# Storing each 128-token output tile with one DMA in place of four

## The chip, the cores and the metric

The kernel runs on one core of a Trainium2 chip. Times are device microseconds (us) of one execution, and each time quoted is the median of all executions of that kernel in its rounds. A span is the length of one profiled execution as the profiler sees it, 1.8 to 2.1 us below the device time of the same execution; all profiled executions shown were in the fast state. In the views, PE is TensorE (PEld its weight loads), DVE is VectorE, ACT is ScalarE, POOL is GpSimd and SP is SyncE; a q after the name is that engine's queue of instructions. PSUM is the memory that holds the tiles named ps_ in the views, which the matmuls write.

## The reference, cut to what matters

```
p_packed = softmax(p k^T / 8) v             # per batch and head: 32 x 64
attn     = softmax(q p_packed^T / 8) p_packed
x        = attn as 4608 tokens x 512        # 8 batches x 576 tokens
out      = relu(x @ w_in)**2 @ w_out        # 4608 x 512 float32, 9.44 MB
```

Only the last line's output and its way to memory are touched by the change.

Of the kernel before, what the change touches and what calls it, by code (L numbers as in the profile page):

```python
# [18 lines left out]
JT = 18  # L19
# [84 lines left out]
def kernel_impl(tc, q, k, v, p, w_in, w_out, out):  # L104
    nc = tc.nc
    B, H, S, Dh = q.shape
# [11 lines left out]
    NT = TOK // P  # L118

    with ExitStack() as ctx:  # L120
# [41 lines left out]
        def cast(eng, dst, src):  # L162
            if eng is nc.scalar:
                nc.scalar.copy(dst, src)  # L164
            else:
                eng.tensor_copy(dst, src)  # L166
# [290 lines left out]
        EH = NE // 2  # L457
# [16 lines left out]
        def out_tile():  # L474
            return opool.tile([P, 2, NE], F32, name="o_sb")

        def store(t, src, eng=None, e0=0, e1=NE):
            for i in range(4):
                b, j = divmod(t * 4 + i, JT)
                dst = out[b * S:(b + 1) * S, e0:e1].rearrange("(a j) e -> j a e", j=JT)[j]  # L480
                (eng or nc.sync if i % 2 else nc.sync).dma_start(dst, src[32 * i:32 * i + 32])
# [8 lines left out]
        def f2_last_out(hf, eng):  # L490
            if hf == 0:
                ob[NT - 1] = out_tile()
            o = ob[NT - 1][:, hf, :EH]
            cast(eng, o, po[NT - 1, hf][:, :EH])
            store(NT - 1, o, nc.scalar, hf * EH, (hf + 1) * EH)

        def f2_mm(t, fb):
            n0 = (t * P) % (2 * S)
# [5 lines left out]
        def f2_out(t, eng):  # L504
            ob[t] = out_tile()
            o = ob[t][:, 0]
            cast(eng, o, po[t])
            store(t, o)
# [53 lines left out]
        def prod_out(t, n, eng):  # L562
            ps = po[t, n not in (2, 4, 6)].rearrange("p (u e) -> p u e", u=2)
            if n == 1:
                ob[t, 0] = out_tile()
            if n == 4:
                ob[t, 1] = out_tile()
            o = ob[t, 0 if n in (1, 2, 3, 6) else 1]
            o = o[:, :, :EH] if n in (1, 2, 7) else o[:, :, EH:]
            if n in (1, 3, 4, 7):  # L570
                cast(eng, o, ps)
            else:
                eng.tensor_tensor(out=o, in0=ps, in1=o, op=ALU.add)  # L573
            if n in (6, 7):
                for u in range(2):
                    store(t + u + (2 if n == 7 else 0), ob[t, n - 6][:, u])
# [189 lines left out]
        def f2_last_steps():  # L766
            res = []
            t = NT - 1
            for hf in range(2):
                for fb in range(NFB):  # L770
                    st = [stage([("PE", 0.11, lambda fb=fb, hf=hf: f2_last(hf, fb))])]
                    end = fb == NFB - 1
                    if end:
                        st.append(stage([("DVE", 0.35, lambda: f2_last_out(0, V)) if hf == 0 else ("ACT", 0.38, lambda: f2_last_out(1, A))]))
                    res.append(Step(f"F2.{t}.{hf}.{fb}", st, g_ready([t], [fb]), [(bk(t, hf), 1)] if fb == 0 else [("osb", 1)] if end and hf == 0 else [],
                                    [(bk(t, hf), 1, f"F2.{t}.{hf}.0")] + ([("osb", 1, f"F2.{t}.0.{fb}")] if hf else []) if end else []))
            return res
# [154 lines left out]
```

## The kernel before: what the change touches

A q load puts token `a*18 + j` of a batch (a = 0..31, j = 0..17) on partition a, position j. A transpose on DVE then makes columns in the order `j*32 + a`. So a tile of 128 columns holds four values of j with 32 tokens each, and on the output side its 128 partitions are four groups of 32 rows; rows of one group are 18 rows apart in the output. The kernel stores each group by a DMA of its own:

```
S, JT, P, NE, EH = 576, 18, 128, 512, 256           # 36 tiles of 128 tokens
opool = tile_pool(name="opool", bufs=3)              # three output buffers of two tiles

def store(t, src, eng=None, e0=0, e1=NE):
    for i in range(4):
        b, j = divmod(t * 4 + i, JT)
        dst = out[b * S:(b + 1) * S, e0:e1].rearrange("(a j) e -> j a e", j=JT)[j]
        (eng or nc.sync if i % 2 else nc.sync).dma_start(dst, src[32 * i:32 * i + 32])
...
def f2_out(t, eng):                                   # tiles 0 to 14, one at a time
    ob[t] = out_tile(); o = ob[t][:, 0]
    cast(eng, o, po[t]); store(t, o)
...
# tiles 15 to 34: groups of four (15, 19, 23, 27, 31), seven products each; two tiles are
# stored after product 6 and two after product 7
# tile 35: in two halves of 256 columns, with nc.scalar for two of each half's four DMAs
```

SP (`nc.sync`) only issues DMAs. The order of all work on each engine is fixed in the kernel. All loads but three are issued by GpSimd (81 of 84). The page counts loads and stores together, in the DMA row's mean busy share of the core's 16 DMA engines.

The softmax here doesn't subtract the row's maximum and nothing guards it: scores larger than these inputs give would overflow.

## Time and profile before

| | before |
|---|---|
| device time, median of 3 runs | 250.09 us (248.85 to 252.26) |
| span of the profiled run (an execution of 251.01 us) | 249.2 us |
| TensorE (PE) busy | 226.0 us, 91% |
| last matmul ends | 241.71 us |
| stretch after it | 7.4 us |
| stores issued | 144 by SP, 4 by ACT |

The prediction shows most of the lines to read. Two more answers are needed for the comparison: the row of the table by stretches in which the loads end (columns: length; busy us and instructions of PE, PEld, DVE, ACT, POOL; clock; DMA share; GB/s), and the view of the output tensor, with the time that SP needs for an issue (min/median/max in ns).

```profile
60.00:80.00 20.00, 18.66 (x180) 10.21 (x182) 16.23 (x27) 16.30 (x30) 8.54 (x18) 1.00 1.05 174
...
L481 SPq DMA_DIRECT2D out_dram<-o_sb x144: 314/422/1790, 48.5 to 246.6; - x144
```

### The profile page before, as it was taken

The page shows a single profiled execution, that of the slowest core. Times are in us where ns is not written, and L with a number is a line of the kernel's source. Part 1 is how long each engine was busy: PE and PEld are TensorE (multiplying, and loading weights), DVE is VectorE, ACT ScalarE, POOL GpSimd, SP SyncE. Part 2 cuts the span into 40 slices and gives each one's busy share as a digit, 9 for nine tenths or more (in the row PEclk, how much of TensorE's full clock was granted, in tenths as well). Part 3 has the DMA queues.
Part 4 walks back from the last instruction along what each step waited for, and adds up shares of the span by engine and source line. Part 5 has one row for each costly group of instructions (what it writes and reads, how often), then busy time and mean ns, then how long its engine had stood idle before and what let it go on. Part 6 is the DMA issues. An engine that isn't in the chain of part 4 may idle for free.

```text
span 249.2 us, 5356 instructions
## 1 busy us (share of the span) xinstructions
PE 226.0 (91%) x2079; PEld 161.1 (65%) x2096; DVE 185.8 (75%) x325; ACT 158.0 (63%) x273; POOL 60.3 (24%) x120
## 2 busy tenths in 40 slices
PE   0667999999899999999999999999999999999980
PEld 0523745476544666666646778887787888888860
DVE  3774557895898896679787989988898798768410
ACT  2467556988687676776788788887875756400010
POOL 7596668473076003261010000000000000000000
PEclk9999999999999999999999999999999999999997
DMA  6999999999989963799711010033004101504243
GB/s 214 200 145 183 205 201 208 204 226 241 197 124 192 248 134 56 117 165 214 144 45 42 3 42 3 0 82 92 3 21 120 32 3 39 130 1 105 66 108 103
DMA packets 27160, 29.01 MB, mean 116 GB/s; under 512 B 5760, under 2 KB 18816, under 8 KB 27136
## 3 DMA queue, kind: packets, MB, share of 16 engines
q0 software_dynamic: 19472, 17.99, 45.7%
q1 hardware_dynamic: 7328, 9.97, 14.7%
q10 hardware_dynamic: 336, 0.72, 0.8%
q8 instruction: 16, 0.26, 0.4%
q14 instruction: 8, 0.07, 0.1%
HBM read 37.22 MB, written 9.44 MB: 187 GB/s over the span
## 4 chain that ended last, share of the span: by engine, by line
PE 74%; DMA 15%; POOL 3%; DVE 2%; issue 1%; ACT 1%; SPq 0%; POOLq 0%
PE ps_o L560 24%; PE ps_h L417 20%; PE ps_o L501 15%; DMA q_b<-in_q_dram 7%; DMA k_b<-in_k_dram 4%; DMA p_b<-in_p_dram 3%; PE ps_m L354 3%; PE ps_a L283 3%; PE ps_h L426 3%; PE ps_s L379 2%; POOL v_r L238 1%; PE ps_pp L316 1%; PE ps_s L391 1%; DVE qT L267 1%; DMA out_dram<-o_sb 1%
## 5 line engine op out<-in xcount | busy, mean ns | idle before, releaser
L445 ACT ACTIVATE r<-ps_h 128x576 bf16<-128x576 f32 x99 | 63.7, 650 | 26.6 <-PE ps_h L417 24.6
L417 PE MATMUL ps_h<-a,M 128*128 128x288 bf16 x448 | 71.0, 286 | 0.2
L501 PE MATMUL ps_o<-w_out_b,gT 128*128 128x512 bf16 x193 | 54.6, 379 | 0.9 <-issue 0.5
L417 PEld LDWEIGHTS <-M 128*128 128x128 bf16 x448 | 43.6, 98 | 16.3
L452 DVE TENSOR_TENSOR gT<-r 128x1152 bf16<-128x1152 bf16 x64 | 46.8, 748 | 6.8 <-ACT r L445 3.8
L560 PEld LDWEIGHTS <-wS 128*128 128x128 bf16 x320 | 31.0, 98 | 4.7 <-issue 0.4
L501 PEld LDWEIGHTS <-gT 128*128 128x128 bf16 x240 | 22.2, 98 | 17.0 <-issue 3.4
L560 PE MATMUL ps_o<-wT,wS 128*128 128x256 bf16 x240 | 30.4, 273 | 0.0
L164 ACT CAST M<-ps_m 128x1024 bf16<-128x1024 f32 (+1 forms) x26 | 23.0, 915 | 6.8 <-PE ps_m L354 4.9
L238 POOL DMA_DIRECT2D v_r<-in_v_dram x32 | 19.0, 598 | 33.3 <-DVE wT L525 16.9
L560 PEld LDWEIGHTS <-gT 128*128 128x128 bf16 x240 | 23.3, 98 | 3.8 <-issue 0.4
L267 DVE STREAM_TRANSPOSE qT<-q_b 128x1152 bf16<-128x1152 bf16 (+1 forms) x18 | 21.9, 1229 | 3.7 <-DMA q_b<-in_q_dram 3.5
L164 ACT COPY o_sb<-ps_o 128x512 f32<-128x512 f32 (+1 forms) x15 | 8.6, 572 | 22.7 <-PE ps_o L560 19.6
L560 PE MATMUL ps_o<-w_out_b,gT 128*128 128x256 bf16 x160 | 20.9, 273 | 0.0
L283 PE MATMUL ps_a<-pT_bd,kT 128*128 128x128 bf16 x128 | 11.0, 242 | 9.5 <-DVE kT L273 8.6
L166 DVE COPY o_sb<-ps_o 128x512 f32<-128x512 f32 (+1 forms) x20 | 13.4, 672 | 8.1 <-PE ps_o L560 3.6
L283 PEld LDWEIGHTS <-kT 128*128 128x128 bf16 x128 | 9.3, 109 | 11.9 <-DVE kT L273 9.0
L166 DVE CAST M<-ps_m 128x1024 bf16<-128x1024 f32 (+1 forms) x10 | 11.2, 1118 | 7.5 <-PE ps_m L354 6.8
L386 ACT ACTIVATE e<-ps_s,rD 128x576 bf16<-128x576 f32 (+1 forms) x18 | 12.2, 687 | 6.8 <-PE ps_s L379 6.8
L573 DVE TENSOR_TENSOR o_sb<-ps_o,o_sb 128x512 f32<-128x512 f32 x15 | 10.3, 690 | 6.2 <-PE ps_o L560 5.0
L379 PE MATMUL ps_s<-qT,pq_bd 128*128 128x288 bf16 x64 | 11.4, 304 | 2.8 <-DVE qT L267 1.5
L273 DVE STREAM_TRANSPOSE kT<-k_b 128x320 f32<-128x320 f32 (+1 forms) x32 | 13.1, 450 | 1.2 <-DMA k_b<-in_k_dram 0.9
(72 smaller groups left out, 304.4 us busy)
## 6 DMA issues: line engine op xcount, KB each, us to landing
out_dram<-o_sb SPq DMA_DIRECT2D x140, 64.0 KB, 1.7
k_b<-in_k_dram POOLq DMA_DIRECT2D x14, 288.0 KB, 8.5
q_b<-in_q_dram POOLq DMA_DIRECT2D x14, 288.0 KB, 8.7
v_r<-in_v_dram POOLq DMA_DIRECT2D x16, 160.0 KB, 8.2
v_r<-in_v_dram POOLq DMA_DIRECT2D x16, 128.0 KB, 7.4
w_in_b<-in_moe_w_in_dram POOLq DMA_DIRECT2D x8, 256.0 KB, 8.7
w_out_b<-in_moe_w_out_dram POOLq DMA_DIRECT2D x8, 256.0 KB, 9.2
k_f<-in_k_dram ACTq DMA_DIRECT2D x1, 576.0 KB, 4.7
```

The source lines that it names most:

```text
L164: nc.scalar.copy(dst, src)
L166: eng.tensor_copy(dst, src)
L238: nc.gpsimd.dma_start(self.vr[32 * i:32 * i + 32, h0:h1, :n * D], src[:, :, J0[i] * D:(J0[i] + n) * D])
L267: nc.vector.transpose(self.qT[:, qd, :, j0 * 32:j1 * 32].rearrange("p dh (j a) -> p j dh a", a=32), self.t.qb[qd][:, j0 * D:j1 * D].rearra ...
L273: nc.vector.transpose(self.kT[:, qd, :n * P].rearrange("p (g jp a) -> p jp g a", jp=4, a=32)[:, i:i + 2], self.t.kb[qd][:, J0[i] * D:(J0[i ...
L283: nc.tensor.matmul(ps[:, g * P:(g + 1) * P], lhsT=self.kT[:, qd, g * P:(g + 1) * P].bitcast(BF16).rearrange("p (t two) -> p two t", two=2) ...
L379: nc.tensor.matmul(ps[:, c], lhsT=self.pq[:, blk(qd, dh)], rhs=self.qT[:, qd, dh, n0:n0 + HALF], start=(dh == 0), stop=(dh == 1))
L417: nc.tensor.matmul(ps[:, c, :HALF], lhsT=a.M[:, qd, fb * FB:(fb + 1) * FB], rhs=a.a2[:, qd, c * HALF:(c + 1) * HALF], start=(qd == 0), sto ...
L445: nc.scalar.activation(dst, src, ACT.Relu)
L452: eng.tensor_tensor(out=gT[:, fb - 1:fb + 1, o:o + S], in0=r, in1=r, op=ALU.mult)
L501: nc.tensor.matmul(po[t], lhsT=gT[:, fb, n0:n0 + P], rhs=w_out_b[:, fb, :], start=(fb == 0), stop=(fb == NFB - 1))
L560: nc.tensor.matmul(ps[:, u * EH:(u + 1) * EH], lhsT=lhs, rhs=rhs, start=(n in (1, 2, 4) and kk == 0 and u == 0), stop=(kk == KB - 1 and u ...
```

## The change

It is meant to save SP's time: one issue for each tile that lies in one batch (32 of 36; the last of them keeps its two halves), in place of four. Below, such a store is called wide, and one of 32 rows narrow.

```
 def store(t, src, eng=None, e0=0, e1=NE):
+    if t * 4 // JT == (t * 4 + 3) // JT:
+        b, j = divmod(t * 4, JT)
+        dst = out[b * S:(b + 1) * S, e0:e1].rearrange("(a j) e -> j a e", j=JT)[j:j + 4]
+        (eng or nc.sync).dma_start(dst, src)
+        return
     for i in range(4):
...
-            store(NT - 1, o, nc.scalar, hf * EH, (hf + 1) * EH)
+            store(NT - 1, o, nc.scalar if hf else None, hf * EH, (hf + 1) * EH)
```

## The prediction

k is the number of DMA engines that one DMA runs on, and completions are packets of 4 bytes: in the trace of the kernel before SP's queue has 2,336 of them, 16 for each of its 146 DMAs. That the new pattern would run on four engines was the assumption at this point, and so was the 125 ns, taken between the two clusters named there. Engines 0 to 3 are its name for these four.

> **What bounds the kernel now.** I read the page first: busy shares, then the 40 slices, then the DMA queues.
>
> ```profile
> PE 226.0 (91%) x2079; PEld 161.1 (65%) x2096; DVE 185.8 (75%) x325; ACT 158.0 (63%) x273; POOL 60.3 (24%) x120
> ...
> PE   0667999999899999999999999999999999999980
> ...
> DMA  6999999999989963799711010033004101504243
> ...
> q1 hardware_dynamic: 7328, 9.97, 14.7%
> ```
>
> TensorE is the bound from the fifth slice to the last but two. Two more things are to be seen: the DMA engines are full for the first 14 slices (87 us), while the loads run, and mostly idle after slice 20; and in the last slice TensorE is idle while DMA works. The table by stretches says how long that lasts (columns: length; busy us and instructions of PE, PEld, DVE, ACT, POOL; clock; DMA share; GB/s):
>
> ```profile
> 40.00:60.00 20.00, 18.98 (x203) 11.86 (x205) 17.48 (x33) 16.36 (x29) 12.41 (x25) 1.00 1.21 221
> ...
> 220.00:242.00 22.00, 21.71 (x199) 19.21 (x197) 11.46 (x18) 2.55 (x5) 0.00 (x0) 1.00 0.30 75
> 242.00:249.20 7.20, 0.00 (x0) 0.00 (x0) 0.00 (x0) 0.17 (x1) 0.00 (x0) 0.82 0.38 100
> ```
>
> The chain of waits stops at ACT's last copy, at 242.17, so it does not explain the last 7 us. The timeline of the end does:
>
> ```profile
> 237.23 9.81 SPq L481 DMA_DIRECT2D out_dram<-o_sb  x20
> ...
> 241.79 0.37 ACT L164 COPY o_sb<-ps_o 128x256 f32<-128x256 f32 x1 [2.95 <-DMA out_dram<-o_sb]
> 242.20 0.80 ACTq L481 DMA_DIRECT2D out_dram<-o_sb  x2
> ```
>
> SP's queue issues the last 20 stores one after another, 0.49 us each, until 247.04, though all data is ready at 242.16. (The release named for that copy is doubtful: the last matmul ends at 241.72, which fits as well.) About 1.3 us of landing and 1.0 us of closing follow. So the tail is bound by SP's issues, and the change aims at it. I also looked for a place where a load is critical[...]:
>
> ```profile
> 61.92 1.38 DVE L267 STREAM_TRANSPOSE qT<-q_b 128x1152 bf16<-128x1152 bf16 x1 [2.06 <-DMA q_b<-in_q_dram]
> ...
> 63.36 0.66 PE L379 MATMUL ps_s<-qT,pq_bd 128*128 128x288 bf16 x4 [1.08 <-DVE qT L267]
> ```
>
> There is one: a q load issued at about 51 us is waited for by DVE, and TensorE waits for DVE. After 66 us no engine waits long for a load.
>
> [...]
> [...] SP issues 146 DMAs in all (144 stores, two loads) with 144·32 rows for stores (2,048 B, or 1,024 B in four), 256 for p and 128 for k, 4,992 packets of data. 7,328 − 4,992 = 2,336 = 146·16, so each used 16 engines; their patterns begin with 32 or 128. No DMA of before begins with a smaller size, so the case k < 16 is not shown yet.
> [...] single 2,048 B packets take 84 to 160 ns, median 105, in two clusters at 85 and near 150[...].
> [...]
>
> **The change, part by part.** Of 36 tiles, 4 straddle two batches (4, 13, 22, 31) and keep four DMAs. 31 whole tiles become one DMA each, and the last tile two halves of 128 rows of 1,024 B. SP's and ACT's issues fall from 148 to 49. No compute instruction changes, nor its order.
>
> *Removed.* In the tail SP issues 4 + 3 + 1 instead of 20. Starting at 237.23 with perhaps 0.6 us for an issue of more rows (estimate from 0.42 for one of before), SP is through at about 241.5, and ACT issues the last half at 242.2. Were all 16 engines used, the end would be 242.2 + 0.6 + 1.5 landing + 1.0 closing = 245.3, a gain of 3.9 us: 246.2 in device time, which is 0.9 above the span (250.09 against 249.2).
>
> *Added.* The new output pattern is 4 x 32 x 512: its slowest dimension is 4, the source's 128. [...] A tile is 128 packets: 8 per engine before, 32 on each of four engines now. [...] I take 125 ns: 32 · 0.125 = 4.0 us a tile, 65 GB/s (2.7 us at 85 ns, 4.8 at 150).
>
> *The tail then.* SP's first issues for the last four groups of four tiles stand at 185.19, 209.35, 225.00 and 237.23; 225.00 had its first packet at 225.81, so 0.8 us later. At 4.0 us a tile, group 23 runs from 210.2 to 226.2, when group 27 is due; that runs to 242.2, past the arrival of group 31 at 238.0. There follow the straddling tile (8 packets an engine, 0.8 us), three whole tiles (12 us) and two halves (64 packets of 1,024 B at about 60 ns, 3.8 us): 258.8. With 0.5 us of receipt and 1.0 of closing the span is 260.3, the time 261.2. At 85 ns no backlog arises: 238.0 + 0.5 + 3·2.7 + 2.9 + 1.5 = 251.0, or 252 to 253 since SP reaches the whole tiles after four narrow issues (1.9 us). At 150 ns: 210.2 + 19.2 + 19.2 + 1.0 + 14.4 + 4.8 + 1.5 = 270.3, time 271.2. The three output buffers also come free later, but the engines that then wait lie behind the same DMA backlog, so I add nothing for it.
>
> *The load stage.* Tiles 2, 0 and 1 are stored from 48.54 to 56, inside the full stretch before 62. On engines 0 to 3 they take 96 packets instead of 24: 72 · 0.125 = 9.0 us more, interleaved with the loads[...]. Perhaps half of it falls before the critical q load: 4 us, which TensorE pays in full unless its other waits shrink. Later stores come 7 us apart beside loads with slack: nothing. I give this +3 us.
>
> **Rivals.**
> *A: sixteen engines after all* (the pattern rearranged below the kernel): 246.2. For it: 128 source rows. Against: the built program carries the pattern as 4 x 32 x 512, source 128 x 1 x 512. I give it 12%.
> *B: four engines, but at 85 ns and with the loads untouched*: the backlog only replaces SP's queue, about 253. For it: [...] slices 20 to 40 show a DMA share of about 0.2 to 0.3 on 16 engines, in the groups' stage, which on four is about 0.8 to 1.2 and so just about fits. Some 15%.
> *C: four engines[...], full backlog from 209 on*: 265 to 275.
> *D: issue cost*. A 128-row issue could cost far more of SP's time than 0.6 us. SP issues 48 stores in place of 144, so each may take three times the 0.47 us of before and SP is no busier.
>
> **Range and chances.** Centre 261.2 + 3 = 264 for the main case; A and B pull the median to 262. Low 250 leaves out A and the best of B, high 274 leaves out the worst of C. Over 2% faster means under 245.1, which even A misses: 4%. Within 2% (245.1 to 255.1) are A and B: 20%. Slower: 76%.
>
> **What would show it.** SP's queue would have 4,992 data packets plus 16·(16 + 2) + 32·k completions: 5,408 with k = 4, 5,792 with k = 16. The landing of a whole tile should be 4 to 6 us from its issue, against a median of 1.7 before; DVE's wait for q near 62 us should grow by 2 to 6 us; after TensorE's last matmul 10 us or more should remain, with a low DMA share (four of 16 engines is 0.25), where SP no longer issues. I am wrong if k is 16, if four engines move more than 100 GB/s, or if the buffers hold TensorE long before the end.

## The result, and the profile after

The changed kernel takes 259.83 us (259.76 to 262.36, 4 runs) against 250.37 us of the kernel before (4 runs); the ratio is 1.040, with a 95% interval of 1.030 to 1.049. It is slower. A ratio here is the mean time of one kernel's fast runs over that of the other's of the same rounds, so it is not quite the ratio of the medians beside it.

The page of the changed kernel, in its busy shares, slices and queues:

```profile
PE 226.2 (88%) x2079; PEld 160.6 (62%) x2096; DVE 186.0 (72%) x325; ACT 157.7 (61%) x273; POOL 60.2 (23%) x120
...
PE   0679998993989999999999999999999999999900
PEclk9999999999799999999999999999999999999975
DMA  7999999999349953799621010022015002212321
...
q1 hardware_dynamic: 5408, 9.96, 12.3%
```

TensorE does the same work, 226.2 us against 226.0. What grew is its idle time, in two places: slice 10 (58 to 64.5 us), with a lower clock in the slice after it, and the end, where two slices are empty in place of one. The queue row tells why: SP's queue has 5,408 packets. The 4,992 packets of data are unchanged, and in place of 2,336 completions (packets of 4 B) the trace has 416: 18 DMAs (16 narrow stores and two loads) at 16 each are 288, and the 32 wide ones at 4 each are 128. The sum is 5,408 exactly; the wide store at 147.15 us, which comes alone, ends with four of them, from 150.89 to 151.51. While the last burst of wide stores runs (12.6 us), four packets of data are on their way at once for 9.5 us and never more than seven, where the kernel before has up to 16 or 17 in its last burst. So each wide DMA ran on four DMA engines.

The table by stretches, for the rows that answer to those of before:

```profile
40.00:60.00 20.00, 18.56 (x176) 11.34 (x177) 15.68 (x31) 17.04 (x31) 10.70 (x22) 1.00 1.21 215
60.00:80.00 20.00, 14.76 (x139) 8.31 (x142) 13.44 (x19) 11.22 (x18) 7.01 (x15) 0.91 0.67 120
...
220.00:242.00 22.00, 22.00 (x204) 19.69 (x202) 13.17 (x21) 2.33 (x5) 0.00 (x0) 1.00 0.23 80
242.00:258.10 16.10, 3.05 (x28) 2.49 (x26) 0.42 (x1) 0.55 (x2) 0.00 (x0) 0.69 0.24 76
```

In the stretch from 60 to 80 TensorE lost 3.9 us (14.76 against 18.66). From 220 to 242 it lost nothing, so the output buffers never held TensorE up late in the kernel. After 242 it works 3.05 us more, and then 13.0 us remain, against 7.4 before. The DMA share there is 0.24: about four engines of 16.

The first place, in the timeline (start, length, what, and in brackets the idle time before it and what ended it):

```profile
62.65 1.38 DVE L267 STREAM_TRANSPOSE qT<-q_b 128x1152 bf16<-128x1152 bf16 x1 [5.14 <-DMA q_b<-in_q_dram]
...
64.09 1.14 PE L379 MATMUL ps_s<-qT,pq_bd 128*128 128x288 bf16 x4 [4.15 <-DVE qT L267]
```

DVE waits 5.14 us for the q load in place of 2.06, and TensorE 4.15 in place of 1.08. The same four matmuls then take 1.14 us in place of 0.66: the clock records show half clock from 63.88 us for 3.41 us. The load itself is slower, as the chain of waits shows for the kernel before and for early3 (described below):

```profile
51.36 10.54 DMA q_b<-in_q_dram
```

```profile
49.63 13.25 DMA q_b<-in_q_dram
```

In the changed kernel the slower of the two q loads issued there takes 12.7 us, and in the seven traces of kernels whose early stores use 16 engines and whose transposes are unchanged (middle, tail, tail64, early16w, all16w, twoq, relu7) it takes 10.5 to 10.8.

The second place, SP's and ACT's queues at the end, with ACT's last copy between them:

```profile
240.57 1.72 SPq L486 DMA_DIRECT2D out_dram<-o_sb  x4
...
242.34 3.12 SPq L481 DMA_DIRECT2D out_dram<-o_sb  x4
...
245.13 0.37 ACT L164 COPY o_sb<-ps_o 128x256 f32<-128x256 f32 x1 [2.95 <-PE ps_o L492]
245.53 1.15 ACTq L481 DMA_DIRECT2D out_dram<-o_sb  x1
```

SP is now done with its issues at 245.46, long before the end: the row of issues is gone. In its place SP waits for data to land, which the view of SP's waits puts at 10.8 us, the longest 6.4:

```profile
SPq L932 <- DMA out_dram<-o_sb: 10.8, 3, 6.4
```

By the packets in the trace, the last burst of stores runs from 243.51 to 256.12, 12.6 us: three tiles of 32 packets of 2,048 B on each of four engines, and 64 packets of 1,024 B.

To add the two places up, I matched the matmuls of both traces in order. Before the first store they already differ: the changed kernel's run is 2.3 us ahead at the matmuls that start at 24.3 us in the kernel before. The two kernels are the same up to there; the profiled run of before simply began late (the other kernels below, identical there too, reach this point 1.2 to 2.3 us before it). The changed kernel is 2.4 ahead at 46 us, 0.7 behind at 63.4, 2.2 behind at 64.8, 3.3 behind at 68.6, and stays 3.3 behind until the last matmul. So it lost 5.7 us in this one stretch, and 5.6 us more after the last matmul (13.0 less 7.4). Not all of the 5.7 us is the change's: a kernel that comes earlier to the q load waits longer for it, and the seven kernels just named lose 0.1 to 1.0 us against the profiled run of before in the same stretch (2.5 where the clock fell, in tail and all16w). Medians, which do not depend on that one run, give less.

### The profile page after: what moved, and what is told of

It is laid out like the page before. It is cut to its first block, busy times and chain, and to the rows that moved or that the text cites.

```text
span 258.1 us, 5198 instructions
## 1 busy us (share of the span) xinstructions
PE 226.2 (88%) x2079; PEld 160.6 (62%) x2096; DVE 186.0 (72%) x325; ACT 157.7 (61%) x273; POOL 60.2 (23%) x120
## 3 DMA queue, kind: packets, MB, share of 16 engines
q1 hardware_dynamic: 5408, 9.96, 12.3%
## 4 chain that ended last, share of the span: by engine, by line
PE 69%; DMA 15%; POOL 5%; issue 3%; DVE 2%; ACT 1%; ACTq 0%; POOLq 0%
PE ps_o L565 24%; PE ps_h L417 18%; PE ps_o L506 14%; DMA v_r<-in_v_dram 7%; DMA w_in_b<-in_moe_w_in_dram 4%; DMA k_b<-in_k_dram 4%; PE ps_m L354 3%; PE ps_s L379 2%; PE ps_a L283 2%; PE ps_o L492 1%; PE ps_pp L316 1%; POOL w_in_b L246 1%; PE ps_h L426 1%; PE ps_s L391 1%; POOL w_out_b L250 1%
## 5 line engine op out<-in xcount | busy, mean ns | idle before, releaser
L445 ACT ACTIVATE r<-ps_h 128x576 bf16<-128x576 f32 x99 | 63.7, 650 | 27.0 <-PE ps_h L417 25.0
L506 PEld LDWEIGHTS <-gT 128*128 128x128 bf16 x240 | 22.3, 98 | 18.6 <-issue 3.4
```

The lines of the kernel that those rows point to most:

```text
L445: nc.scalar.activation(dst, src, ACT.Relu)
L506: nc.tensor.matmul(po[t], lhsT=gT[:, fb, n0:n0 + P], rhs=w_out_b[:, fb, :], start=(fb == 0), stop=(fb == NFB - 1))
```

## The experiments

The theory: two separate losses, both because four DMA engines carry what 16 carried before. (1) Early stores take four engines from the loads, and one q load comes late. (2) The last tiles drain slowly. Rivals: the late load was chance; a backlog of all earlier groups lengthens the end, as the prediction had it; a DMA of 256 KB is slow in itself, on whatever engines; SP's issues never bound the end.

Ratios leave out the runs in the slow state: one each of middle and all16w, two of early16w. All runs were correct by the comparison with the reference, except early16w. The comparison cannot tell rows of one batch apart, though: in the reference they differ by some 4 parts in a million of their size. all16w has its rows in wrong places. The order was therefore checked in the simulator, with q, k, v and p twelve times as large, for which neighbouring rows differ by 18%: the kernel before, the changed kernel, natural and relu7 came within 0.6%, all16w did not (18%).

**early3.** Only tiles 0, 1 and 2 are stored wide (four engines).

```
-            if t * 4 // JT == (t * 4 + 3) // JT:
+            if t < 3 and t * 4 // JT == (t * 4 + 3) // JT:
```
and tile 35 as in the kernel before.

> Only tiles 0, 1 and 2 are stored by one DMA each on four engines (k = 4); all others, the last too, as before. Theory (two separate costs, one of them here): the stores take engines 0 to 3 from the loads, so DVE's wait for the q load near 62 us is 4 to 6 us in place of 2.1, TensorE's wait behind it 3 to 5 us in place of 1.1, a short drop of the granted clock follows, and the time is 253 to 256 us against about 250 for the kernel before; the tail after the last matmul stays at 7 to 8 us. Rival (the longer wait in the changed kernel was chance, all of the loss is in the tail): 250, waits as before. Completions of SP's queue: 4992 + 16 x 134 + 4 x 12 / 4, that is 134 DMAs of 16 and 3 of 4: 7148 packets.

Measured: 254.76 us against 250.36, ratio 1.019 (1.010 to 1.028). The timeline of early3:

```profile
62.90 1.38 DVE L267 STREAM_TRANSPOSE qT<-q_b 128x1152 bf16<-128x1152 bf16 x1 [4.94 <-DMA q_b<-in_q_dram]
...
64.34 1.14 PE L379 MATMUL ps_s<-qT,pq_bd 128*128 128x288 bf16 x4 [3.95 <-DVE qT L267]
```

The waits are those of the changed kernel, half clock follows (6.8 us of it here), and the stretch after the last matmul is 7.5 us as before. SP's queue has 7,148 packets, as forecast. Three stores are enough for the whole first loss, 4.4 us by the medians, and the late load was not chance.

**middle.** Only tiles 3 to 30 are stored wide.

```
-            if t * 4 // JT == (t * 4 + 3) // JT:
+            if 3 <= t < 31 and t * 4 // JT == (t * 4 + 3) // JT:
```
and tile 35 as in the kernel before.

> Only tiles 3 to 30 are stored by one DMA each on four engines; tiles 0 to 2 and 31 to 35 as before. Theory: these stores cost nothing, because the loads beside them have slack and each group's four tiles (about 12.4 us of transfer) are done before the next group's come: 250 us, within 1 us of the kernel before. Rival (a backlog of earlier groups is what lengthened the end, as the prediction had it): 253 us or more, with the last 20 narrow stores landing late.

Measured: 250.08 us against 250.36, ratio 0.9998 (0.997 to 1.003; 20 runs). These 25 wide stores cost nothing, and gain nothing, and no backlog of theirs reaches the end. The changed kernel's packets show why: the four tiles of group 23 run from 213.84 to 226.21, 12.4 us, and group 27's first packet comes at 229.5.

**tail.** Only tiles 32, 33, 34 and 35 are stored wide.

```
-            if t * 4 // JT == (t * 4 + 3) // JT:
+            if t >= 31 and t * 4 // JT == (t * 4 + 3) // JT:
```

> Only tiles 32, 33, 34 and the two halves of 35 are stored by one DMA each on four engines; all before as in the kernel before. Theory: transfer of the last tiles on four engines takes about 12.6 us from the first wide issue, so the stretch after the last matmul is about 13 us in place of 7.5 and the time 255 to 256.5 us. Rival 1 (the tail is long only through a backlog of earlier groups): 250 or less. Rival 2 (fewer issues pay after all): 246 to 248.

Measured: 255.58 us against 250.36, ratio 1.018 (1.012 to 1.024). The stretch after its last matmul:

```profile
241.20:253.60 12.40, 0.00 (x0) 0.00 (x0) 0.00 (x0) 0.37 (x1) 0.00 (x0) 0.70 0.22 82
```

It is 12.4 us in place of 7.4, at a DMA share of 0.22 and 82 GB/s. So the end is slow without any earlier wide store. By the medians the three parts come to 4.4 − 0.3 + 5.2 = 9.3 us; the whole change costs 9.5.

**tail64.** As tail, with two DMAs of 64 rows for a tile.

```
-                dst = ...rearrange("(a j) e -> j a e", j=JT)[j:j + 4]
-                (eng or nc.sync).dma_start(dst, src)
+                for i in (0, 2):
+                    dst = ...rearrange("(a j) e -> j a e", j=JT)[j + i:j + i + 2]
+                    (eng or nc.sync).dma_start(dst, src[32 * i:32 * i + 64])
```

> As tail, but each of the last tiles is stored by two DMAs of 64 rows, whose pattern begins with 2. Theory (k is the size of the slowest dimension[...]): two engines carry all, 3 x 128 x 0.5 = 192 packets of 2 KB at 84 ns and 128 of 1 KB at 46 ns on each, 16.1 + 5.9 = 22 us: stretch after the last matmul about 22 to 23 us, time 264 to 266. Rival 1 (another pair of engines for each DMA, four in all): as tail, 255 to 256. Rival 2 (16 engines): 247 to 250. Completions of SP's queue fall by 2 for each DMA that has 2.

Measured: 265.74 us (2 runs) against 249.63, ratio 1.063 (1.053 to 1.073). The stretch after its last matmul:

```profile
239.50:262.80 23.30, 0.00 (x0) 0.00 (x0) 0.00 (x0) 0.37 (x1) 0.00 (x0) 0.59 0.12 44
```

Halving the slowest dimension to 2 halves the rate (44 GB/s in place of 82) and the share (0.12, two engines of 16), and SP's queue has 7,088 packets: 4,992, 16 for each of 130 DMAs, and 2 for each of 8. Two DMAs for a tile did not bring four engines: by the share of 0.12 both took the same two. More issues of the same bytes made it slower, so what counts is the number of engines. The median packet still takes 84 ns.

**early16w.** As early3, but to consecutive rows, in wrong places, so that the pattern is 128 x 512.

```
 def store(t, src, eng=None, e0=0, e1=NE):
+    if t < 3:
+        nc.sync.dma_start(out[t * P:(t + 1) * P], src)
+        return
```

> As early3, but the three early tiles go to 128 consecutive rows of the output, so that the one DMA of 256 KB has the pattern 128 x 512 and uses 16 engines (result wrong on purpose: the rows are in the wrong places). Theory (the loss of early3 is that four engines carry the stores): 250 us, DVE's wait for q 2 to 2.7 us and TensorE's 1 to 2.2 as in the kernel before. Rival (one DMA of 256 KB takes more from the loads than four of 64 KB, whatever the engines): 254 to 255 as early3.

Measured: 249.99 us against 249.63, ratio 0.9999 (0.997 to 1.003). One of its 20 runs took 1,303 us, which nothing here explains; it is not among the fast ones. The result is not a number in places, since some rows were never written. Its timeline:

```profile
60.47 1.38 DVE L267 STREAM_TRANSPOSE qT<-q_b 128x1152 bf16<-128x1152 bf16 x1 [2.27 <-DMA q_b<-in_q_dram]
...
61.91 0.66 PE L379 MATMUL ps_s<-qT,pq_bd 128*128 128x288 bf16 x4 [1.28 <-DVE qT L267]
```

The same bytes in the same three DMAs at the same time, on 16 engines (SP's queue has 7,184 packets: 4,992 and 16 for each of 137 DMAs), cost nothing. So the size of a DMA is not the fault; the four engines are. (The rows lie side by side here and 18 rows apart in early3, so the addresses changed as well. They are an unlikely cause: the median packet takes 84 ns in the changed kernel and 86 in all16w, and tail64 changes the engines alone.)

**all16w.** All tiles to consecutive rows by one DMA each (wrong places).

```
 def store(t, src, eng=None, e0=0, e1=NE):
+    (eng or nc.sync).dma_start(out[t * P:(t + 1) * P, e0:e1], src)
+    return
```

> All 36 tiles go to consecutive rows by one DMA each on 16 engines (result wrong on purpose, rows in the wrong places); nothing else is changed against the changed kernel. Theory: the change would have paid with 16 engines: the stretch after the last matmul 3.2 to 3.9 us in place of 7.5, 246 to 247 us (ratio 0.983 to 0.987). Rival (SP's issues were not what bound the end): 250.

Measured: 245.58 us against 249.63, ratio 0.984 (0.981 to 0.988). Its issues (count, KB each, median us to landing) and its end:

```profile
out_dram<-o_sb SPq DMA_DIRECT2D x35, 256.0 KB, 2.3
```

```profile
236.92 3.56 SPq L479 DMA_DIRECT2D out_dram<-o_sb  x5
...
241.89 0.35 ACTq L479 DMA_DIRECT2D out_dram<-o_sb  x1
```

A whole tile lands 2.3 us after its issue, and 3.1 us remain after the last matmul. An issue takes 0.33 us at the median, where a wide one on four engines takes 0.54 and a narrow one 0.42. The idea of the change is worth 1.6% if its DMAs run on 16 engines. This time, like those of twoq and relu7 below, lies 0.3 to 0.6 us under what was expected.

**twoq.** The kernel before, narrow stores only; part of the last ones is moved from SP to ACT.

```
-                (eng or nc.sync if i % 2 else nc.sync).dma_start(dst, src[32 * i:32 * i + 32])
+                on_act = t == NT - 3 or t == NT - 1 and (i % 2 or e0)
+                (nc.scalar if on_act else nc.sync).dma_start(dst, src[32 * i:32 * i + 32])
```

> The kernel before with narrow stores only; tile 33, half of the first half of tile 35 and the second half of it are issued by ACT in place of SP. Theory (SP's row of issues bound the end of the kernel before): SP and ACT are both through at about 244, the stretch after the last matmul is 4.5 to 5.5 us in place of 7.5, 247.5 to 248.5 us. Rival (data or landing bound it): 250.

Measured: 246.92 us against 249.63, ratio 0.988 (0.982 to 0.994). The ends of the two queues:

```profile
235.96 7.16 SPq L482 DMA_DIRECT2D out_dram<-o_sb  x13
...
240.67 1.80 ACTq L482 DMA_DIRECT2D out_dram<-o_sb  x4
```

SP is through at 243.1 and ACT at 242.5, and 5.1 us remain after the last matmul in place of 7.4. That SP's row of issues bound the end of the kernel before is thereby shown, since nothing but the issuing queue was changed.

**natural.** A first attempt to have 16 engines with rows in their right places: the q transposes of batches 1 to 7 write their columns in the order of the tokens, so that a tile is 128 consecutive rows.

```
+                cols = self.qT[:, qd].rearrange("p dh (a j) -> p j dh a", j=JT)   # batches 1 to 7
                 nc.vector.transpose(cols, ...)
...
+            if t > 4:
+                (eng or nc.sync).dma_start(out[t * P:(t + 1) * P, e0:e1], src)
+                return
```
and tiles 0 to 3 and the half of tile 4 that belongs to batch 0 in narrow stores; the other half of tile 4 takes one DMA of 64 rows.

> The q transpose of batches 1 to 7 writes its columns in the order of the tokens, so every tile from 5 on is 128 consecutive rows of the output and its one DMA has the pattern 128 x 512 on both sides; tiles 0 to 3 and half of 4 stay narrow. Theory (four engines are the fault, not the size of a DMA): k = 16, a tile lands within 2.5 us of its issue, SP is done at about 4 us after the last matmul's tile, tail 3.5 to 4.5 us in place of 7.5, no cost for the loads: 246 to 247 us. Rival 1 (a DMA of 128 rows is slow in itself): 255 or more. Rival 2 (DVE's transpose is slower when it writes with a step of 18 columns: 1.38 us would grow): 249 to 255, visible in the mean of the transposes.

Measured: 295.3 us, ratio 1.179 (1.172 to 1.185). The transposes in the groups of before and then of natural (count | busy us, mean ns):

```profile
L267 DVE STREAM_TRANSPOSE qT<-q_b 128x1152 bf16<-128x1152 bf16 x14 | 19.0, 1364 | 3.2 <-DMA q_b<-in_q_dram 3.2
```

```profile
L269 DVE STREAM_TRANSPOSE qT<-q_b 128x1152 bf16<-128x1152 bf16 x14 | 71.4, 5122 | 0.0
```

The second rival held, far beyond its range of 249 to 255 us: a transpose that writes with a step of 18 columns takes 5.1 us in place of 1.4, 52 us more on DVE. The stores did what the theory said: 2.3 us to landing, and 3.3 us after the last matmul.

**relu7.** The order is changed elsewhere, and only for the last batch: its ReLUs read PSUM in the order of the tokens and write plainly. Tiles 32 to 35, and half of 31, then are consecutive rows in their right places; all others are stored as before.

```
+            if a.b == B - 1:
+                dst = r.rearrange("p (a c j) -> p a c j", c=2, j=JH)
+                src = src.rearrange("p c (j a) -> p a c j", a=32)
...
 def store(t, src, eng=None, e0=0, e1=NE):
+    if t >= NT - 4:
+        (eng or nc.sync).dma_start(out[t * P:(t + 1) * P, e0:e1], src)
+        return
+    if t == NT - 5:
+        nc.sync.dma_start(out[t * P + 64:(t + 1) * P], src[64:])
-    for i in range(4):
+    for i in range(2 if t == NT - 5 else 4):
...
+            store(NT - 1, o, nc.scalar if hf else None, hf * EH, (hf + 1) * EH)
```

> The kernel before, but the ReLUs of the last batch read PSUM in the order of the tokens (step of 32 elements), so tiles 32 to 35 are consecutive rows of the output and each takes one DMA on 16 engines in its right place; half of tile 31 likewise with 64 rows. Theory: stretch after the last matmul 3.2 to 4 us in place of 7.5; the ReLUs of that batch no slower than 650 ns on ACT: 245.5 to 246.5 us against 250, as all16w. Rival (reading PSUM with a step is slow, as writing with a step was for the transposes): 16 ReLUs grow, 248 to 255 us.

Measured: 245.18 us (244.7 to 245.42, 6 runs) against 250.48, ratio 0.979 (0.975 to 0.983). ReLUs on ACT, among them those of the last batch, and the end of SP's queue:

```profile
L448 ACT ACTIVATE r<-ps_h 128x576 bf16<-128x576 f32 x99 | 63.8, 650 | 26.5 <-PE ps_h L417 24.6 <-DVE gT L455 0.3
```

```profile
236.65 1.93 SPq L482 DMA_DIRECT2D out_dram<-o_sb  x4
...
239.94 0.35 ACTq L482 DMA_DIRECT2D out_dram<-o_sb  x1
```

The mean stays at 650 ns (63.8 us in all, 63.7 before), and the last twelve, which read with a step, take 644 to 652 ns each, so reading PSUM with a step cost nothing. 3.2 us remain after the last matmul. This kernel beats both others.

## Why the prediction was right, and where it was off

The measured 259.83 us lies in the range of 250 to 274 and 2.2 us below the centre of 262. The sign and its causes were right; two sizes were off, in opposite directions, so that the centre was this near is luck.

- *What bounds the end before* (SP's row of issues): right. twoq moves issues alone and gains; all16w makes an end at 245.58 where "were all 16 engines used" gave 246.2.
- *Four engines* (k = 4, the size of the slowest dimension): assumed there, and right by the count of packets, 5,408; tail64 shows the same for a slowest dimension of 2 (7,088 packets, a share of 0.12). Rival A is out.
- *Issue cost*: estimated at 0.6 us; a wide issue takes 0.54 us at the median. Rival D is out.

```profile
L481 SPq DMA_DIRECT2D out_dram<-o_sb x32: 527/537/945, 46.2 to 244.5; - x32
```

- *"I take 125 ns"*: this step failed. Packets of the wide stores take 84 ns at the median; four tiles in a row take 12.4 us, 3.1 us each, not 4.0, and 85 GB/s, not 65. Nearly all the slow packets are the first 16 of a burst, most of them 112 to 994 ns, over some 1.5 us; five to eight later ones exceed 110 ns. A tile that comes alone pays this start by itself: the one at 147.15 us takes 4.4 us, so the 4.0 was about right for it, for another reason. That the 150 ns cluster would be the likelier one was the estimate, and no lasting slowdown of that kind is seen. The 150 ns cluster belongs to the narrow stores: 40% of the packets of 2,048 B in the kernel before take over 130 ns, but in all16w's DMAs of 128 rows only 0.2%; why, no run shows.
- *The backlog from group 23 on* therefore did not arise. middle shows it directly (0.9998). The stretch after the last matmul was predicted at 260.3 − 241.7 = 18.6 us; it is 13.0. The whole of the tail was put at +11.1 us (261.2 less 250.1); tail measures +5.2. (The 0.9 us that the prediction adds to a span is the median of before less the span of one execution that took 251.01; within one execution the difference is about 2 us. This changes no argument.)
- *The tail without backlog* (the 85 ns case, 252 to 253) came nearer, but was too short: it leaves 10.3 to 11.3 us after the last matmul, and 12.4 (tail) and 13.0 were measured. Three of its terms were too small: the first packet comes 1.2 us after the first wide issue where 0.8 was assumed, the burst takes 12.6 us where three tiles and two halves sum to 3 · 2.7 + 2.9 = 11.0 (the slow start), and closing took 1.9 us after the last data where 1.5 was assumed.
- *The load stage*: the right load and the right wait were named, and the step "DVE's wait should grow by 2 to 6 us" holds (+3.1, of which 2.2 is the slower load, 12.7 us for 10.5; the rest goes with the lead of 2.3 us). The term of +3 us was too small: early3 measures +4.4. The fall of the clock after the wait was not in the working at all; how much of the 4.4 it makes, no run separates. Nor does the length of TensorE's wait alone decide it here: half clock followed 4.15 us (the changed kernel), 3.95 (early3), 1.97 (tail) and 1.96 (all16w), and did not follow 1.08 (before) or 2.20 (middle).
- *Buffers add nothing, later stores add nothing*: right (TensorE is busy 22.00 of 22 us from 220 on; middle). One copy of ACT's, at 237.27 us, did wait for a buffer: ACT idled 7.34 us before it, where it idled 6.40 before the same copy in the kernel before. TensorE did not wait for it.

So the true account is +4.4 and +5.2, where the main case had +3 and +11, drawn down to 262 by the chances given to A and B. The step that failed is the 125 ns and the backlog built on it; that the centre was so near is owed to the load term, too small by 1.4 us, and to that averaging.

What stays open: why the first 1.5 us of a burst on four engines are so slow; no run shows it.

## What to carry to other kernels

Before merging DMAs, look at the outermost dimension of the merged pattern on both sides. Here it, not the number of bytes, went with the number of DMA engines: 4 in the output with 128 in the source gave four engines, 2 with 64 gave two, and 32 or 128 on both sides gave 16 (256 KB ran on four in early3 and on 16 in early16w). The number of packets in the queue's row tells afterwards how many engines worked: 5,408 in place of 7,328 here. A saved issue is worth something only where the issuing engine is the last to finish; here that was the last five tiles (all16w 0.984, twoq 0.988) and nowhere else (middle 0.9998). If order stands in the way of a pattern with 128 rows outermost, change the order where a step costs nothing (here a read of PSUM by a ReLU, 644 to 652 ns against a mean of 650, where a DVE transpose that writes with a step of 18 columns took 5.1 us against 1.4), and only for the tiles that matter.
